# Delta-rule attention with a gated MLP on one core: triangular inverses in 16x16 blocks for the first three groups, weight decoding at a lower rank, more split buffers and held-back output products at the end

## The chip, the cores and the metric

The kernel runs on one core of a Trainium2 chip. A core has a matrix engine (TensorE, PE in the profile; its weight loads are PEld), a vector engine (VectorE, DVE), a scalar engine (ScalarE, ACT), GpSimd (POOL) and a queue processor that here issues all the transfers (SyncE, SP). The metric is the device time of one execution in microseconds. Shown are the median of three runs and, apart from it, one execution with a profile. Each engine works through its own list of instructions in order; an instruction that has to wait holds up all that stand behind it on its engine.

## The reference

```python
k_n = k / (np.linalg.norm(k, axis=-1, keepdims=True) + 1e-06)
for t in range(S):                       # S = 768; B, H, D = 4, 8, 48
    y[:, :, t] = q[:, :, t] @ state      # per head, state is 48 x 48
    v_old = state.T @ k_n[:, :, t]
    state = state + beta[t] * outer(k_n[:, :, t], v[:, :, t] - v_old)
x = y.transpose(0, 2, 1, 3).reshape(B, S, H * D)         # 4 x 768 x 384
h = np.maximum(x @ w_in, 0.0)                            # 384 -> 1024
u, v = h[..., :512], h[..., 512:]
v_n = (v - mean(v)) / np.sqrt(var(v) + 1e-06)
v_s = np.einsum('ts,bsd->btd', w_spatial, v_n) + b_spatial[None, :, None]
return (u * v_s) @ w_out                                 # 512 -> 384
```

(The inner products are written here as matrix products; in the reference they are `einsum`s over all heads.)

## The kernel before

**Recurrence.** The 768 positions are cut into 12 chunks of 64. Two batches with their 16 heads run at a time, so there are 24 steps: 0 to 11 for batches 0 and 1, 12 to 23 for batches 2 and 3. Inside a chunk, the recurrence is the inverse of a 64x64 unit triangular matrix per head, built from K K^T, the key norms and beta. Four steps form a group, and `prep(g)` prepares a group's inverses: matmuls `kk` (tile `ke`, or `bn` at the start), a copy into the tile `xt`, half copies (L402), a 32x32 block transpose on DVE into `la` (L407), small operations on 128x32 tiles for the norm (L413 to L422: `gd`, `sq`, `t0`, `nl`, `dv`), a scaling of `la` (L423), then the *lanes*. The lanes invert all the 32x32 triangular blocks of the group at once: one block a partition row, one column j after the other, each a product (L439) and a sum (L444) over all rows that are known so far. Rows 0 to 15 are DVE's (`ps`, in PSUM), rows 16 to 31 GpSimd's (`wl`). A copy (L450) and a transpose (L451) put the result back into `xt`. `widen(s)` then makes a 64x64 inverse of two 32x32 inverses and the block between them: a transpose `tn` (L470), 16 matmuls, a scaling `pi` (L487), 16 matmuls, two copies (L491). A matmul in f32 shows as two records in the trace, one in fp32r as one.

`step(s)` is the recurrence itself: the old value from the state (`s,bn`), a subtraction (L542), the product with the inverse (`bn,xt`), the copy `w` (L571), the product into the state (`w,bn`), its sum (L584) and the outputs (`bn,s` and `pt,w`). `kqt` makes the masked Q K^T (`pt`, L516), `scale_v` the scaled v (L502), and `load(s)` brings `bn` (k, q, v, k of a step, 896 KB) for one of two buffers.

**MLP.** Every second step finishes 128 rows of x for two batches. `convert` splits them into high and low parts; `mlp_v`, `norm_v`, `split_v` and `mlp_u` make v, its norm, its split into tiles `vf`, and u. `gate(b)` starts once a batch's 768 rows are there: for three column ranges `mlp_g` multiplies with w_spatial, adds the bias `bbc` (L735), multiplies with u (L738) and splits the result (L740, L741); `mlp_o` multiplies with w_out, and the result is copied (L756) and stored. Products of weights and data are three matmuls (high x high, high x low, low x high).

**Weights** arrive as 64-bit floats. `load_f64` decodes w_in in six blocks on DVE (L288, L294, L296), ACT (L290 to L293, L297) and GpSimd (L298, L299), and `split_w` splits them (L278, L279).

**The order** is written by a planner. `P.add(engine, duration, function, reads, writes, pr=...)` registers each operation; `run` takes operations one by one with planned durations: of the engine that can start earliest it takes the ready operation with the lowest rank `pr`. The emitted order is then each engine's list. Ranks: the recurrence has the step number (0 to 23), the widening 250 + s, kqt 300 + s, the MLP from 5000 on, prep of group 0 has -925 to -922, that of the later groups 1,000 + 100 g and more. Decoding on DVE has `pre(pr)`, -930, while the weights' rank is under 1000. Pools hand out buffers: `full` (six `vf` tiles), `raw` (seven), `g` (the gated tiles, `g0` and from step 23 on `xt0`, `xt1`), `pm` (PSUM banks).

Of the kernel before, what the change touches and what calls it, by code (L numbers as in the profile page):

```python
# [27 lines left out]
EPS = 1e-6  # L28
NRAW = 7
# [4 lines left out]
class Op:  # L34
    __slots__ = ("i", "eng", "dur", "fn", "pr", "deps", "out", "n", "acq", "rel", "give", "start", "end", "lag", "port")
# [15 lines left out]
class Plan:  # L51
# [35 lines left out]

    def run(self):
# [3 lines left out]
        est = {}  # L92
# [12 lines left out]
        while left:  # L105
# [36 lines left out]
            o.end = t + o.dur + o.lag  # L142
            for p, h in o.rel:
# [28 lines left out]
def delta_rule_gated_mlp(  # L172
# [21 lines left out]
    bbc = new("bbc", SEQ)  # L194
# [4 lines left out]
    ptm = [new(f"pt{i}", NS * 64) for i in range(2)]  # L199
    bnd = [new(f"bn{i}", 1792) for i in range(2)]  # L200
# [9 lines left out]
    la, wl, ke2 = (tagged(t, 1024) for t in ("la", "wl", "ke"))  # L210
# [3 lines left out]
    raw_ = lambda h: h.get(lambda u: tagged(f"vr{u}", DH))  # L214
    full_ = lambda h: h.get(lambda u: tagged(f"vf{u}", 2 * DH, F32R))
# [22 lines left out]
    P.pool("raw", range(NRAW))  # L238
    P.pool("full", range(NFULL))
# [17 lines left out]
    P.add("POOL", 1.0, lambda: nc.gpsimd.memset(wl, 0.0), wr=["wlo", "whi"], pr=-10)  # L257
# [43 lines left out]
    def pre(pr):  # L301
        return -930 if pr < 1000 else pr

    def weights():
        for idx in range(2 * NK):
# [3 lines left out]
            t1 = lambda h1=h1: h1.get(lambda u: tagged(f"vf{u}", 1024))  # L309
# [9 lines left out]
        ld(bbc, b_sp.unsqueeze(0).broadcast_to([128, SEQ]), wr=["bbc"], pr=950)  # L319
        for idx in range(NT // 2):  # L320
# [3 lines left out]
            ld(lambda t=t: v3(t()[:, 0:1536], SEQ), w_sp[idx * 256 : idx * 256 + 256].rearrange("(a p) n -> p a n", p=128), wr=[key], pr=900 + idx, acq=[("st", h)], lag=4.0)  # L324
# [32 lines left out]
    def prep(g):  # L357
        base = 1925 + g * 100 if g else 0
        for s4 in range(GP):
# [10 lines left out]
            ld(ke, k_t[s], wr=[kk_], pr=30 + s if g else -20 + s4)  # L370
# [7 lines left out]
            P.add("PE", 0.55, kk, rd=[kk_], wr=bk + [("kk", s)] + [("x", k % (2 * GP), q) for k in (range(s, s + GP) if s4 == 0 else (s,)) for q in ("d0", "o0", "z1", "d1")], pr=400 + s, acq=acq)  # L378
# [13 lines left out]
        ld(bl_[g % 2], b_l[g], wr=[("bl", g % 2)], pr=40 + g if g else -5)  # L392
# [11 lines left out]
        for a in range(2):  # L404
# [3 lines left out]
            out=v3(la, 32), in_=xg()[:, :, 0:32].rearrange("p b c -> p c b")), rd=xp("d0") + [("za", 0), ("za", 1)], wr=["la"] + xp("z1"), pr=base - 930)  # L408
        la3 = v3(la, 32)
# [3 lines left out]
        P.add("DVE", 0.1, lambda: nc.vector.tensor_copy(out=gd, in_=dg), rd=["la"], wr=["gd"], pr=p0, port=True)  # L413
# [13 lines left out]
        P.add("ACT", 0.2, lambda: nc.scalar.copy(out=pr_[:, 0 : 15 * 33 + 1 : 33], in_=dv[:, 0:16]), rd=["dv"], wr=["wp"], pr=p0)  # L427
        P.add("POOL", 0.15, lambda: nc.gpsimd.tensor_copy(out=wl[:, 16 * 33 : 31 * 33 + 1 : 33], in_=dv[:, 16:32]), rd=["dv"], wr=["whi"], pr=p0)
        P.add("DVE", 0.1, lambda: nc.vector.transpose(out=nn[g % 2], in_=n_l), rd=["nl"], wr=[("nn", g % 2)], pr=p0 + 1)
        w3, wp = v3(wl, 32), v3(pr_, 32)  # L430

        def lanes(eng, key, w, t_, i0, j):
# [5 lines left out]
            cost = dve_t(n * m) if eng == "DVE" else 0.1 + 1.85e-3 * n * m  # L438
# [349 lines left out]
    for s in range(NP):  # L788
# [9 lines left out]
        if s % GP == GP - 1 and g + 2 < NG:  # L798
            prep(g + 2)
# [69 lines left out]
```

## Time and profile before

| | us |
|---|---|
| median of 3 runs (555.1 to 558.07) | 557.56 |
| profiled execution, its own time | 559.17 |
| its span, first to last instruction | 557.5 |
| PE busy | 447.9 |
| DVE busy | 276.3 |
| ACT busy | 237.5 |
| POOL busy | 267.4 |

The span was at a mean granted TensorE clock of 0.916. Busy times of different engines overlap. A busy TensorE can still be slow: the clock that it was granted is a column of its own in the views by stage. In rows that list an instruction, the bracket at the end is the idle time of its engine just before it, and what ended that. In rows of groups, the busy total and the mean in ns come first, then the idle time before, and who ended it.

### The profile page before, as it was taken

The page shows a single profiled execution, that of the slowest core. Times are in us where ns is not written, and L with a number is a line of the kernel's source. Part 1 is how long each engine was busy: PE and PEld are TensorE (multiplying, and loading weights), DVE is VectorE, ACT ScalarE, POOL GpSimd, SP SyncE. Part 2 cuts the span into 40 slices and gives each one's busy share as a digit, 9 for nine tenths or more (in the row PEclk, how much of TensorE's full clock was granted, in tenths as well). Part 3 has the DMA queues.
Part 4 walks back from the last instruction along what each step waited for, and adds up shares of the span by engine and source line. Part 5 has one row for each costly group of instructions (what it writes and reads, how often), then busy time and mean ns, then how long its engine had stood idle before and what let it go on. Part 6 is the DMA issues. An engine that isn't in the chain of part 4 may idle for free.

```text
span 557.5 us, 19319 instructions
## 1 busy us (share of the span) xinstructions
PE 447.9 (80%) x8520; PEld 402.9 (72%) x8520; DVE 276.3 (50%) x690; ACT 237.5 (43%) x505; POOL 267.4 (48%) x372
## 2 busy tenths in 40 slices
PE   3000497959688998887979789898999997999996
PEld 3000496748677876777778679787999996998996
DVE  3599447688866489756887584213320021100100
ACT  3762642275428548664524213343323576014111
POOL 2189565758324466537456334344245141448442
PEclk9999999988869699885598798978999999899999
DMA  8601233321432363025302240210000000001001
GB/s 279 243 1 57 63 101 127 112 96 46 134 136 82 101 204 87 29 70 171 112 2 96 77 141 32 88 58 29 9 29 28 29 2 1 1 29 52 6 29 56
DMA packets 16020, 42.49 MB, mean 76 GB/s; under 512 B 3393, under 2 KB 7617, under 8 KB 15937
## 3 DMA queue, kind: packets, MB, share of 16 engines
q1 hardware_dynamic: 15936, 41.27, 22.4%
q8 instruction: 66, 1.08, 0.8%
q14 instruction: 18, 0.14, 0.1%
HBM read 35.36 MB, written 4.72 MB: 72 GB/s over the span
## 4 chain that ended last, share of the span: by engine, by line
PE 63%; DVE 20%; ACT 5%; issue 5%; DMA 4%; POOL 1%; SPq 1%; POOLq 0%; ACTq 0%; DVEq 0%
PE ps L355 63%; DVE ps L444 4%; DVE prod L439 4%; DMA bn<-in_bun 2%; DMA vf<-in_w_in 2%; DVE xt L451 2%; DVE pt L516 1%; DVE vf L296 1%; DVE la L407 1%; DVE ut L294 1%; ACT gt L653 1%; ACT vr L668 1%; ACT w L571 1%; SPq L250 1%; DVE la L423 1%
## 5 line engine op out<-in xcount | busy, mean ns | idle before, releaser
L355 PE MATMUL ps<-wsp_h,vf 128*128 128x256 f32 x576 | 122.4, 295 | 5.1 <-ACT vf L676 2.5
L355 PEld LDWEIGHTS ps<-wsp_h,vf 128*128 128x128 f32 x576 | 97.2, 196 | 7.7 <-ACT vf L676 2.7
L355 PE MATMUL ps<-wsp_l,vf 128*128 128x256 f32 x288 | 83.3, 289 | 0.0
L735 DVE TENSOR_TENSOR gt<-ps,bbc 128x512 f32<-128x512 f32 x24 | 16.6, 691 | 104.7 <-PE ps L355 104.7
L738 POOL TENSOR_TENSOR gt<-gt,ut 128x512 f32<-128x512 f32 x24 | 30.8, 1284 | 71.4 <-DVE gt L735 70.0
L444 DVE TENSOR_TENSOR ps<-ps,prod 128x192 f32<-128x192 f32 (+8 forms) x180 | 59.3, 329 | 5.4
L439 DVE TENSOR_TENSOR prod<-ps,la 128x192 f32<-128x192 f32 (+8 forms) x180 | 57.8, 321 | 5.4
L355 PEld LDWEIGHTS ps<-wsp_l,vf 128*128 128x128 f32 x288 | 56.7, 197 | 0.0
L677 POOL TENSOR_TENSOR vf<-vr,vf 128x512 fp32r<-128x512 f32 x24 | 30.6, 1288 | 51.0 <-ACT vf L676 51.0
L355 PE MATMUL ps<-ke 48*64 48x64 f32 x704 | 18.9, 262 | 41.2 <-DVE pt L516 38.4
L355 PEld LDWEIGHTS ps<-ke 48*64 48x64 f32 x704 | 15.7, 168 | 46.7 <-DVE pt L516 38.9
L355 PE MATMUL ps<-bn 48*64 48x64 f32 x832 | 23.7, 271 | 22.0 <-DVE pt L516 12.4
L502 POOL TENSOR_TENSOR bn<-bn,nn 128x384 f32<-128x384 f32 x24 | 20.9, 873 | 37.2 <-DMA bn<-in_bun 21.9
L355 PEld LDWEIGHTS ps<-bn 48*64 48x64 f32 x832 | 20.3, 179 | 24.4 <-DVE pt L516 12.7
L402 POOL COPY xt<-xt 32x1024 f32<-32x1024 f32 x17 | 17.6, 1035 | 40.4 <-DVE xt L451 20.8
L355 PE MATMUL ps<-wout_h,g 128*128 128x384 f32 x96 | 27.4, 348 | 3.0 <-ACT g L740 2.2
L584 DVE TENSOR_TENSOR s<-s,ps 112x384 f32<-112x384 f32 x20 | 11.0, 552 | 36.2 <-PE ps L355 32.9
L571 ACT COPY w<-ps 128x384 f32<-128x384 f32 x24 | 11.4, 477 | 41.1 <-PE ps L355 37.4
L756 ACT COPY ob<-ps 128x384 f32<-128x384 f32 x24 | 11.5, 478 | 41.0 <-PE ps L355 29.6
L355 PE MATMUL ps<-wout_h,xt 128*128 128x384 f32 x96 | 26.6, 343 | 2.1 <-POOL xt L741 1.5
L444 POOL TENSOR_TENSOR wl<-wl,prod 128x28 f32<-128x28 f32 (+3 forms) x84 | 23.8, 283 | 6.3
L439 POOL TENSOR_TENSOR prod<-wl,la 128x28 f32<-128x28 f32 (+3 forms) x84 | 23.1, 275 | 6.3
(142 smaller groups left out, 1099.4 us busy)
## 6 DMA issues: line engine op xcount, KB each, us to landing
bn<-in_bun SPq DMA_DIRECT2D x22, 896.0 KB, 4.7
ke<-in_k_t SPq DMA_DIRECT2D x22, 256.0 KB, 2.9
out<-ob SPq DMA_DIRECT2D x24, 192.0 KB, 1.9
vf<-in_w_in SPq DMA_DIRECT2D x6, 512.0 KB, 9.0
g<-in_w_sp SPq DMA_DIRECT2D x3, 768.0 KB, 4.4
g<-in_w_out SPq DMA_DIRECT2D x4, 384.0 KB, 3.2
bn<-in_bun SPq DMA_DIRECT2D x2, 640.0 KB, 6.3
xs<-xs SPq DMA_DIRECT2D x66, 16.0 KB, 3.1
```

What stands on the lines that cost most here:

```text
L355: nc.tensor.matmul(o, l, r, start=start, stop=stop)
L402: (nc.gpsimd.tensor_copy if eng == "POOL" else nc.scalar.copy)(out=xg()[r, :, o : o + 32], in_=xg()[r, :, i : i + 32])
L439: P.add(eng, cost, lambda: e.tensor_tensor(out=dst if j == i0 else pt, in0=w[:, :n, j : j + 1].broadcast_to([128, n, m]), in1=la3[:, j, j ...
L444: P.add(eng, cost, lambda: e.tensor_tensor(out=dst, in0=dst, in1=pt, op=ALU.add), rd=[pk], wr=[key], pr=p0 + 2)
L451: P.add("DVE", 2.2, lambda: nc.vector.transpose(out=xg()[:, :, 0:32].rearrange("p b c -> p c b"), in_=w3.rearrange("p i t -> p t i")), rd= ...
L502: P.add("POOL", 0.84, lambda: nc.gpsimd.tensor_tensor(out=v, in0=v, in1=n.unsqueeze(2).broadcast_to([128, NS, HD]), op=ALU.mult), rd=[("nn ...
L571: P.add("ACT", 0.48, lambda: nc.scalar.copy(out=v3(w, 192), in_=v3(pc, 512)[:, :, 0:192]), rd=["pc"], wr=[("w", s % 2)], pr=pr)
L584: P.add("DVE", 0.55, lambda: nc.vector.tensor_tensor(out=sv, in0=sv, in1=pv, op=ALU.add), rd=["pc"], wr=["S"], pr=pr)
L677: P.add("POOL", pool_t(512), lambda: nc.gpsimd.tensor_sub(out=full_(f)[:, DH : 2 * DH], in0=raw_(r), in1=full_(f)[:, 0:DH]), rd=[kk, ("vh" ...
L735: P.add("DVE", 0.69, lambda: nc.vector.tensor_tensor(out=gt(), in0=v3(bank(h.unit), 256), in1=bbc[:, th * 256 : th * 256 + 256].unsqueeze( ...
L738: P.add("POOL", pool_t(512), lambda: nc.gpsimd.tensor_mul(out=gt_[t.unit], in0=gt_[t.unit], in1=u_(uh)[:, half * 512 : half * 512 + 512]), ...
L756: P.add("ACT", 0.48, lambda: nc.scalar.copy(out=ob_[t.unit], in_=bank(h.unit)[:, :DM]), rd=[("po", b, th, o)], wr=[("ob", b, th, o)], pr=4 ...
```

## The change

- **16x16 lanes.** For the first three groups (`G16 = 3`) the lanes invert two 16x16 blocks of each row instead of one 32x32 block, all on DVE, with 15 columns instead of 31; GpSimd has no lanes there. The new `widen16(s)` makes the 32x32 inverses of them, per step, ahead of the old `widen(s)`. The group's half copies and memsets behind the lanes go; `widen16` does them per step. ACT copies the block that it needs into `kd` before it is overwritten. `kd` and `tn6` lie in the tile that later holds the bias, whose load moves behind step 11.
- **Decoding later.** `pre` gives -800 instead of -930.
- **The end.** When the last step is done, the two `bn` buffers join the pool `full` and the two `pt` buffers the pool `raw`. Batch 1's split waits for batch 0's gates as before; batch 3's split waits for batch 2's splits instead of batch 2's gates. Output products have a later rank: +135 for batch 1, +8 for batches 2 and 3, +2.5 before.
- **Replanned.** Planned durations are changed all over, transfers share a line of 330 KB a us, and the planner has a model of a TensorE that slows when it is little used. `prep(g + 1)` is registered at the start of group g, behind that group's `widen16`. Every engine's order can change.

```diff
     def pre(pr):
-        return -930 if pr < 1000 else pr
+        return -800 if pr < 1000 else pr
...
+        if g < G16:
+            P.add("ACT", 0.6, lambda: nc.scalar.copy(out=v3(kd, 16), in_=xg()[:, :, 0:16]), rd=xp("d0") + [("za", 0), ("za", 1)], wr=["kd"], pr=410 + g)
...
-        P.add("DVE", 0.1, lambda: nc.vector.tensor_copy(out=gd, in_=dg), rd=["la"], wr=["gd"], pr=p0, port=True)
+        P.add("DVE", 0.24, lambda: nc.vector.tensor_copy(out=gd, in_=dg), rd=["la"], wr=["gd"], pr=p0, port=True)
...
+        def lanes16(j):
+            n, m = j + 1, 15 - j
+            w4 = pr_.rearrange("p (h i t) -> p h i t", h=2, t=16)
+            pt = prod[:, : 2 * n * m].rearrange("p (h a b) -> p h a b", h=2, b=m)
+            dst = w4[:, :, :n, j + 1 : 16]
+            cost = 0.19 + 1.05e-3 * 2 * n * m
+            P.add("DVE", cost, lambda: nc.vector.tensor_tensor(
+                out=dst if j == 0 else pt, in0=w4[:, :, :n, j : j + 1].broadcast_to([128, 2, n, m]),
+                in1=v3(la_, 528)[:, :, 33 * j + 1 : 32 * j + 16].unsqueeze(2).broadcast_to([128, 2, n, m]), op=ALU.mult),
+                rd=["la", "wp"], wr=["wp"] if j == 0 else [("prod", "DVE")], pr=p0 + 2)
+            if j:
+                P.add("DVE", cost, lambda: nc.vector.tensor_tensor(out=dst, in0=dst, in1=pt, op=ALU.add), rd=[("prod", "DVE")], wr=["wp"], pr=p0 + 2)
...
+    def widen16(s):
...
+        P.add("DVE", 0.46, lambda: nc.vector.transpose(out=v3(tn6, 32), in_=x8_()[:, :, 0:32]), rd=zd, wr=["tn6"], pr=pr)
+
+        def e():
+            x8 = x8_()
+            for q in range(NS):
+                for k in range(4):
+                    r = slice(32 * k, 32 * k + 32)
+                    mm(pe[32 * k : 32 * k + 16, q * 16 : q * 16 + 16], kd[r, (b0 + q) * 16 : (b0 + q) * 16 + 16], x8[r, q, 16:32])
+
+        def f():
+            for q in range(NS):
+                for k in range(4):
+                    h = slice(32 * k, 32 * k + 16)
+                    mm(pe[32 * k : 32 * k + 32, 256 + q * 16 : 256 + q * 16 + 16], tn6[h, q * 32 : q * 32 + 32], gi[h, q * 16 : q * 16 + 16])
+
+        P.add("PE", 1.0, e, rd=["kd"] + zd, wr=["pe0"], pr=pr)
+        P.add("ACT", 0.26, lambda: nc.scalar.mul(out=gi, in_=pe[:, 0:128], mul=-1.0), rd=["pe0"], wr=["gi"], pr=pr)
+        P.add("PE", 1.0, f, rd=["gi", "tn6"], wr=["pe0"], pr=pr)
+        P.add("DVE", 0.29, lambda: nc.vector.tensor_tensor(
+            out=x8_()[:, :, 16:32], in0=x8_()[:, :, 16:32], in1=v3(pe[:, 256:384], 16), op=ALU.add), rd=["pe0"], wr=zd, pr=pr)
+        for a in range(2):
+            r = slice(a * 64 + 32, a * 64 + 64)
+            P.add("ACT", 0.37, lambda r=r: nc.scalar.copy(out=x8_()[r, :, 32:64], in_=x8_()[r, :, 0:32]), rd=[("x", sl, "z1")], wr=[("zb", s, a)], pr=pr)
+            P.add("POOL", 0.4, lambda r=r: nc.gpsimd.memset(x8_()[r, :, 0:32], 0.0), rd=[("zb", s, a)], wr=[("zc", s, a)], pr=pr)
...
         if s == NP - 1:
             P.add("X", 0.0, None, rd=[("xs", s // 2)], wr=["pc"], give=[("pm", k) for k in (0, 1, 2, 3, 4)] + [("g", "xt0"), ("g", "xt1")])
+            P.add("X", 0.0, None, wr=[("bn", i, q) for i in range(2) for q in "kqvn"], give=[("full", "bn0"), ("full", "bn1")])
+            P.add("X", 0.0, None, wr=[("pt", 0), ("pt", 1)], give=[("raw", "pt0"), ("raw", "pt1")])
...
-rd=[kk, ("gdone", i // NT - 1)], wr=[("vh", i)]
+rd=[kk] + ([("gdone", 0)] if i // NT == 1 else [("vh", 2 * NT + k) for k in range(NT)] if i // NT == 3 else []), wr=[("vh", i)]
...
-                mlp_o(b, th, o, pr + th * 2 + 2.5 + o * 0.2)
+                mlp_o(b, th, o, pr + th * 2 + (2.5, 135, 8, 8)[b] + o * 0.2)
...
-    prep(1)
     P.add("X", 0.0, None, wr=["pm67"])
     for s in range(NP):
         g = s // GP
+        if s % GP == 0:
+            for k in range(GP if g < G16 else 0):
+                widen16(s + k)
+            if g + 1 < NG:
+                prep(g + 1)
         widen(s)
...
-        if s % GP == GP - 1 and g + 2 < NG:
-            prep(g + 2)
+        if s == GP * G16 - 1:
+            load_bias()
```

More of the change, by code (lines that the diff above doesn't have):

```diff
@@ L34 @@
 class Op:
-    __slots__ = ("i", "eng", "dur", "fn", "pr", "deps", "out", "n", "acq", "rel", "give", "start", "end", "lag", "port")
+    __slots__ = ("i", "eng", "dur", "fn", "pr", "deps", "out", "n", "acq", "rel", "give", "start", "end", "lag", "port", "kb", "took")
 class Hold:
@@ L86, in add, with gate @@
         return o
+    def gate(self, o, t):
+        left, z = o.dur, t
+        while left > 1e-9:
+            k = int(z // GATE)
+            if k not in self.busy:
+                self.busy[k] = 0.0
+                u = self.busy.get(k - 1, 0.0)
+                if z > 100.0 and (u < 0.47 * GATE if k - 1 not in self.slow else u < 0.68 * GATE):
+                    self.slow.add(k)
+            f = 2.0 if k in self.slow else 1.0
+            d = min(left * f, (k + 1) * GATE - z)
+            d = max(d, 1e-6)
+            self.busy[k] += d
+            left -= d / f
+            z += d
+        o.took = z - t
     def run(self):
@@ L91, in run @@
         port = {"DVE": 0.0, "POOL": 0.0}
-        est = {}
+        est, line, self.busy, self.slow = {}, 0.0, {}, set()
         def arm(o):
@@ L142, in run @@
             o.end = t + o.dur + o.lag
+            if o.kb:
+                line = max(line, t) + o.kb / 330.0
+                o.end = max(line + o.lag, o.end)
+            if e == "PE":
+                self.gate(o, t)
+                free[e] = t + o.took
+                o.end = t + o.took
             for p, h in o.rel:
@@ L198, in delta_rule_gated_mlp @@
     tn, pi = new("tn", NS * 32), new("pi", NS * 32)
-    ptm = [new(f"pt{i}", NS * 64) for i in range(2)]
-    bnd = [new(f"bn{i}", 1792) for i in range(2)]
+    ptm = [sb.tile([128, NS * 64], F32, name=f"pt{i}", tag=f"pt{i}") for i in range(2)]
+    bnd = [sb.tile([128, 1792], F32, name=f"bn{i}", tag=f"bn{i}") for i in range(2)]
     wt = [new(f"w{i}", NS * HD) for i in range(2)]
@@ L237, in delta_rule_gated_mlp @@
     P.pool("x", [("xh", "xl")])
-    P.pool("raw", range(NRAW))
-    P.pool("full", range(NFULL))
+    P.pool("raw", [f"vr{i}" for i in range(NRAW)])
+    P.pool("full", [f"vf{i}" for i in range(NFULL)])
     P.pool("u", range(NU))
@@ L437, in lanes @@
             dst = w[:, :n, j + 1 : 32]
-            cost = dve_t(n * m) if eng == "DVE" else 0.1 + 1.85e-3 * n * m
+            cost = 0.19 + 1.05e-3 * n * m if eng == "DVE" else 0.27 + 1.75e-3 * n * m
             P.add(eng, cost, lambda: e.tensor_tensor(
@@ L453, in prep @@
             rd=["wlo", "whi"], wr=xp("d0") + xp("z1"), pr=p0 + 3)
+        if g < G16:
+            if g == G16 - 1:
+                P.add("POOL", 0.6, lambda: nc.gpsimd.memset(wl[:, 512:1024], 0.0), wr=["whi"], pr=p0 + 4)
+            return
         P.add("POOL", 0.6, lambda: nc.gpsimd.memset(wl[:, 512:1024], 0.0), wr=["whi"], pr=p0 + 4)
@@ L642, in mlp_v @@
         st = stt[:, J * 16 : J * 16 + 16]
-        P.add("ACT", 0.75, lambda: nc.scalar.activation(out=raw_(r), in_=bank(h.unit), func=AF.Relu, accum_out=st[:, j : j + 1]),
+        P.add("ACT", 0.82, lambda: nc.scalar.activation(out=raw_(r), in_=bank(h.unit), func=AF.Relu, accum_out=st[:, j : j + 1]),
               rd=[("pv", i)], wr=[("st", i), ("vr", i)], pr=400 + J, rel=[("pm", h)])
@@ L675, in split_v @@
         kk, q = ("vr", i), 440 + i
-        P.add("ACT", 0.6, lambda: nc.scalar.copy(out=full_(f)[:, 0:DH], in_=raw_(r)), rd=[kk, ("gdone", i // NT - 1)], wr=[("vh", i)], pr=q, acq=[("full", f)])
+        P.add("ACT", 0.6, lambda: nc.scalar.copy(out=full_(f)[:, 0:DH], in_=raw_(r)), rd=[kk] + ([("gdone", 0)] if i // NT == 1 else [("vh", 2 * NT + k) for k in range(NT)] if i // NT == 3 else []), wr=[("vh", i)], pr=q, acq=[("full", f)])
         P.add("POOL", pool_t(512), lambda: nc.gpsimd.tensor_sub(out=full_(f)[:, DH : 2 * DH], in0=raw_(r), in1=full_(f)[:, 0:DH]), rd=[kk, ("vh", i)], wr=[("vl", i)], pr=q, rel=[("raw", r)])
```

121 lines of the change are left out of this document (73 added, 48 removed).

## The prediction

> **What bounds the kernel now.** I read the slices of the span first, then the busy time by stage, then the two engines at the start in order of time, then the waits at the end. The slices (tenths busy, 13.9 us each) and the clock:
>
> ```profile
> span 557.5 us, 19319 instructions
> ...
> PE   3000497959688998887979789898999997999996
> ...
> PEclk9999999988869699885598798978999999899999
> ```
>
> TensorE is nearly idle for five slices, 80 to 90% busy at a varying clock up to slice 28, and full after that. The stages are cut at the gaps between groups of four steps; columns are length, then busy time (and instructions) of PE, weight loads, DVE, ACT, POOL, then the granted clock:
>
> ```profile
> 0.00:71.00 71.00, 13.89 (x420) 12.18 (x424) 45.44 (x100) 36.13 (x56) 38.22 (x65) 1.00 0.38 129
> 71.00:98.00 27.00, 23.39 (x800) 21.53 (x800) 17.27 (x43) 9.05 (x21) 14.93 (x20) 1.00 0.34 110
> 98.00:135.00 37.00, 31.12 (x435) 25.01 (x433) 29.37 (x79) 17.80 (x42) 26.04 (x45) 0.91 0.29 90
> 135.00:160.00 25.00, 18.74 (x778) 16.61 (x773) 19.71 (x54) 11.26 (x25) 11.37 (x26) 0.80 0.36 119
> 160.00:181.00 21.00, 19.75 (x532) 16.04 (x530) 12.51 (x34) 13.17 (x30) 6.28 (x7) 0.91 0.35 102
> 181.00:206.00 25.00, 23.36 (x710) 19.32 (x711) 15.33 (x39) 11.35 (x28) 13.36 (x28) 0.80 0.41 134
> 206.00:240.00 34.00, 28.60 (x474) 23.97 (x472) 26.27 (x72) 25.81 (x58) 19.08 (x26) 0.95 0.25 74
> 240.00:395.00 155.00, 135.54 (x3285) 120.48 (x3285) 87.06 (x214) 57.01 (x124) 71.14 (x108) 0.82 0.24 79
> 395.00:466.00 71.00, 71.00 (x519) 67.38 (x519) 13.75 (x38) 34.92 (x83) 27.34 (x20) 1.00 0.06 19
> 466.00:474.00 8.00, 4.71 (x38) 4.29 (x37) 1.32 (x8) 4.95 (x12) 1.27 (x1) 1.00 0.00 0
> 474.00:546.00 72.00, 70.68 (x523) 69.97 (x523) 7.61 (x11) 14.06 (x26) 35.81 (x28) 0.98 0.07 25
> 546.00:557.50 11.50, 7.11 (x38) 6.14 (x37) 0.69 (x1) 1.95 (x4) 2.55 (x2) 0.94 0.14 51
> ```
>
> After the recurrence (395 us) 160 us of MLP work are still queued on PE. So the recurrence doesn't set the end; the sum of PE's work does, plus what PE loses by waiting or by a low clock. I count as lost the stage's length less busy time times clock. The rows at the start show that the clock column misses something there:
>
> ```profile
> 63.11 1.06 PE L355 MATMUL ps<-tn,xt 32*32 32x32 f32 x32 [0.40 <-DVE tn L470]
> ...
> 70.91 1.10 PE L355 MATMUL ps<-bn,xt 64*64 64x48 f32 x32
> ...
> 125.18 0.69 PE L355 MATMUL ps<-tn,xt 32*32 32x32 f32 x32 [1.88 <-DVE tn L470]
> ...
> 240.05 0.69 PE L355 MATMUL ps<-xt,pi 32*32 32x32 f32 x32
> 240.67 0.57 PE L355 MATMUL ps<-w,bn 64*48 64x48 f32 x32
> 241.06 0.63 PE L355 MATMUL ps<-pt,w 64*48 64x64 f32 x32
> ```
>
> The same 32 records take 1.06 us at 63 and 0.69 us at 125: until about 105 us PE runs at 0.65 of its later pace although the column says 1.00. With 0.65 for 71 to 98, the losses are 27 - 23.4 x 0.65 = 12 us, then about 11 (98 to 135, partly slow), 10, 3, 6 and 7 up to 240 (49 in all), 44 from 240 to 395, and 3.3 + 2.7 + 4.8 = 11 behind that. Work from 71 us on is thus 486.5 - 104 = 383 us at full pace.
>
> **The change part by part.** *The start.* DVE, in order of time:
>
> ```profile
> 10.49 1.90 DVE L407 STREAM_TRANSPOSE la<-xt 128x1024 f32<-128x1024 f32 x1 [1.45 <-ACT xt L402]
> ...
> 21.08 0.43 DVE L288 TENSOR_SCALAR ut<-vf 128x512 uint32<-128x512 uint32 x1 [0.85 <-DMA vf<-in_w_in]
> 21.43 0.18 DVE L413 COPY gd<-la 128x32 f32<-128x32 f32 x1
> ...
> 27.55 0.20 DVE L439 TENSOR_TENSOR ps<-ps,la 128x31 f32<-128x31 f32 x1
> ...
> 46.07 0.28 DVE L444 TENSOR_TENSOR ps<-ps,prod 128x112 f32<-128x112 f32 x1
> 46.39 0.26 DVE L439 TENSOR_TENSOR prod<-ps,la 128x96 f32<-128x96 f32 x1
> ...
> 48.31 0.22 DVE L444 TENSOR_TENSOR ps<-ps,prod 128x48 f32<-128x48 f32 x1
> 48.43 0.72 DVE L294 SCALAR_TENSOR_TENSOR ut<-vf,ut 128x512 uint32<-128x512 uint32 x1
> ...
> 58.92 0.18 DVE L444 TENSOR_TENSOR ps<-ps,prod 128x16 f32<-128x16 f32 x1
> 60.35 2.23 DVE L451 STREAM_TRANSPOSE xt<-wl 128x1024 f32<-128x1024 f32 x1 [0.65 <-ACT wl L450]
> ```
>
> The transpose that feeds group 0 ends at 12.39, but its next reader runs at 21.43: the six first decode operations (L288) stand in front of it and wait for the w_in transfers. A second batch of decoding sits inside the lanes from 48.43 to about 58.3. The lower rank of the decoding (-800, behind -925) takes both out: 9.0 and 9.8 us. The lanes themselves take 27.55 to 48.5 and 0.8 more, 21.8 us. The 16x16 lanes are 15 products and 14 sums of 2(j+1)(15-j) elements, 1,360 for all products. From start to start 112 elements take 0.32 us (46.07 to 46.39), which is 0.04 over the duration; 48 elements then take 0.26, so the fit is 0.215 + 0.00094 n: 29 x 0.215 + 0.00094 x 2,690 (all products and sums) = 8.8 us, 13 less.
>
> So for group 0: 12.4; about 5 for the small operations (27.55 - 21.43 = 6.1 now, with pieces of decoding between), 17.5; lanes to 26.2; copy and transpose 3.5 as now (59.1 to 62.6), 29.7. Then the new widening to 32x32: two matmul blocks at the slow pace, 1.6 us each, and 2.1 us for the scaling, sum, copies and memset, 35; then the old widening, 4.5 without group 1's matmuls in between, 39.5. I take **40** for the matmul that is at 70.91 now: **-31** (bounds 36 and 46, since ACT and POOL have decode operations of 0.7 and 1.3 us that can stand ahead of each hop). The price of decoding later:
>
> ```profile
> 39.31 1.28 POOL L298 TENSOR_TENSOR ut<-ut,vf 128x512 f32<-128x512 f32 x1
> ...
> 98.03 1.22 PE L355 MATMUL ps<-win_h,xh 128*128 128x512 f32 x2
> ```
>
> POOL's part (18 operations of 1.3 us) starts at 39 now, behind the POOL lanes that group 0 loses; it can start near 18 and needs 23 us. Its results are read at 98 now, and not before two steps and the conversion of x then, near 62. So it is hidden; if it ends later than that, only MLP work that has no deadline waits. The bias load, moved behind step 11, is read only by the gates of the second half; on SP its wait stands before the next steps' loads, and I cost it at nothing.
>
> *Added matmuls.* widen16 has two blocks of 32 matmuls for each of 12 steps; two records each, so 64 records a block, 24 blocks. No row has this shape. From start to start, 32 records of the old widening take 0.62 us (240.05 to 240.67), and 32 of the four-tile block behind take 0.39. A block then costs 2 x 0.62 = 1.24 (at most 1.32 by the isolated 0.66), 0.78 by the four-tile pace, or 0.62 if half the columns halve the price. The new blocks use four tiles, but of 32 rows as the old widening: I take 1.0, **+24** (15 to 32). The Trainium skill ("TensorEngine Tiling (Array Packing)", Instruction Overhead) says that a matmul pays some 60 cycles whatever its free size and that no tiling should be taken from a size already small; it speaks against this change, and by it the block costs the 1.24, +30 in place of +24. The trace agrees in part: blocks of 32 and of 64 columns both come near 0.62, but the 48-column one goes at 0.39.
>
> *Added on the other engines.* Per step:
>
> ```profile
> L470 DVE STREAM_TRANSPOSE tn<-xt 128x256 f32<-128x256 f32 x24 | 10.6, 440 | 17.9 <-PE ps L355 17.6
> L487 ACT ACTIVATE pi<-ps 128x256 f32<-128x256 f32 x24 | 9.2, 382 | 13.5 <-PE ps L355 13.2
> L491 ACT COPY xt<-ps 32x256 f32<-32x256 f32 x48 | 17.3, 361 | 20.5 <-PE ps L355 20.0
> L458 POOL MEMSET xt<- 32x1024 f32 x12 | 11.5, 954 | 6.6 <-DVE tn L470 2.5 <-DVE gd L413 1.7 <-DVE st L650 1.4
> ```
>
> One more DVE transpose (0.44) and sum (about 0.3), one ACT scaling (under 0.38) and two copies of 0.36, two POOL memsets (at most 0.95 each). They replace the group's two half copies and two memsets. DVE is relieved all the same: 13 us less lanes a group against 3 more. These sit beside PE's work of a group, 33 to 46 us at full pace by the stages above (71 to 135, 135 to 181, 181 to 240); without that cover the chain costs as in the rival below. Behind each new wait stand, on PE, the step's own matmuls; on DVE, the next group's lanes; on POOL, the v scaling.
>
> *Groups 1 and 2.* From 98 to 135 the recurrence stands while DVE finishes group 1's lanes (109 to 120.6) and its transpose; 135 to 160 has the opposite fault, all recurrence and no filler, with the clock at 0.80. Lanes that are 13 us shorter let steps and MLP blocks mix. Of the 49 us lost I take **-10**: nothing at worst, 25 at best.
>
> *Waits for instructions, and the end.*
>
> ```profile
> PE ps L355 <- issue: 12.2, 10, 2.6
> ```
>
> ```profile
> 472.38 0.39 PE L355 MATMUL ps<-wsp_h,vf 128*128 128x256 f32 x1 [2.45 <-ACT vf L676]
> ...
> 550.82 0.62 PE L355 MATMUL ps<-wout_h,xt 128*128 128x384 f32 x2 [0.73 <-POOL xt L741]
> ```
>
> PE waited 12.2 us for nothing that the profile shows, and its longest such waits lie among small matmuls. 24 x 64 = 1,536 more records on 8,520 give 12.2 x 0.18 = 2.2; they fall into the same stretches, so **+3** (0 to 8). At the end, PE waits at 472 for batch 3's split v and at 550 for the last gated tile. With two more split buffers, two more raw ones and output products kept for those places, each batch has six products of 12 matmuls to stand in. Of the 11 us lost I take **-7** (-3 to -9, since the last product, its copy and its store stay). The held products of batch 1 become filler between 240 and 395; that, and planned durations nearer to the trace (small DVE operations 0.24 where 0.1 stood), works on the 44 us lost there. **-4** (-20 to +10): a plan made anew moves every wait, and nothing in the profile says which way.
>
> *The sum.* -31 + 24 - 10 + 3 - 7 - 4 = -25. From the profiled span of 557.5: 532.5. The profiled execution took 559.17, 1.67 more than its span, and the median of the runs shown is 557.56, so a span and a median have the same number here. Forecast **532.5**, with its own range from 518 to 546 (the bounds of start, matmuls and second half, not all at their ends together).
>
> **The rivals.**
>
> *The narrow matmuls cost as much as the wide ones, half of them at low pace.* For it: 32 and 64 columns cost the same above, and 71 to 98 runs at 0.65 with PE 23.4 of 27 us busy. A block is then 1.24 us at full pace and 2.1 at the other, 1.66 on average, 24 of them +40: the sum becomes -9, 548.5. Against it: the block at 0.39. The Trainium skill's rule ("TensorEngine Tiling (Array Packing)", Instruction Overhead), told above, would lead here.
>
> *DVE stays behind the transfers.* If the plan again puts a decode operation ahead of group 0's small ones, they start near 21 as now; 9 us of the 31 are lost: 541. The place is the first reader of the transposed tile. Against it stands the rank.
>
> *The plan frees the second half.* If the fillers close half of the 44 us lost, -22 in place of -4: 514.5. For it: the 395 to 466 stage shows PE full when only MLP work is left.
>
> *Slower: the widening comes into the chain of steps.* Its links (matmul, scaling, matmul, sum, copy, memset) share one tile each for kd, gi, tn6 and one PSUM bank, so one step's must end before the next's starts. By the rows: 1.0 + 0.4 + 1.0 + 0.3 + 0.7 + 0.95 = 4.4 us, 12 times, 52 us, if each starts only when its step needs it. Then the recurrence's first half takes 52 more, PE has no filler since the gates need all twelve steps, and in place of +24 and -10 stands +52: -31 + 52 + 3 - 7 = +17, 574.5. It decides where less than 4.4 us of other PE work lies between two steps. Against it: 33 to 46 us of PE work a group stand there against 4 x 4.4, and the links need nothing from the step before.
>
> *Nothing comes of the early start* would need the recurrence not to feed PE earlier. Since 383 us of work wait from 71 on, and lost time there is 104, I see no room for it.
>
> **How the numbers follow.** Forecast 0.60; equal price 0.15; DVE behind the transfers 0.07; second half freed 0.11; slower 0.07. The range reaches from the freed half to the equal price and a little past both: **511 to 552**; it leaves out the slower rival and the tails, some 0.15. A measurement of this kernel tells about 0.5% from no change, 554.8 to 560.3. Faster 0.60 + 0.07 + 0.11 and 0.11 of the equal price: 0.89. The same: 0.03 of the equal price and 0.01 of the slower rival: 0.04. Slower: 0.07.
>
> **What would show it.** The first reader of the transposed tile before 14 us and the first `bn,xt` matmul near 40: the start. 64-record blocks of 1.0 us at full pace: the added matmuls; 1.24 and 2.1 are the first rival. Gaps between groups (98 to 135 now) of under 15 us: the lanes. Less than 5 us lost behind the recurrence, with output products where the waits were: the end. PE under 80% in the first half, waiting for ACT, DVE or POOL operations of the widening, would be the slower case. The forecast fails if steps begin at 40 but the first half still ends near 206, the early start given back.

## The result, and the profile after

| | before | after |
|---|---|---|
| median, us (4 runs each) | 556.75 | 533.66 |
| range, us | 555.1 to 558.07 | 531.87 to 536.48 |
| profiled execution, us | 559.17 | 533.54 |
| its span, us | 557.5 | 531.7 |
| ratio after/before, 95% interval | | 0.959 (0.954 to 0.964) |

The kernel is 4.1% faster. The forecast was 532.5, the measured median 533.66. The number was right. Of the terms behind it, the added matmuls came near, the start did so only when it is counted as idle time, the end came as forecast, and two others came far from where they were put and cancelled each other. The medians of e7, e9 and e12 further down are over four runs of which one was slow (999.63, 684.53 and 555.47 us); their other runs alone have medians of 544.02, 538.98 and 546.6, and the ratios leave the slow ones out.

The first view is the page of the kernel after: its span, its engines and its slices.

```profile
span 531.7 us, 22308 instructions
...
PE 461.5 (87%) x10056; PEld 413.4 (78%) x10056; DVE 240.3 (45%) x618; ACT 247.0 (46%) x541; POOL 237.4 (45%) x295
...
PE   4336978989799898888598899999999999999997
...
PEclk9999999995955969989699799989999999999999
```

PE starts earlier and is 90% busy or more from slice 24 to the last but one, with no hole at slice 34 as before. It is 13.6 us longer busy (447.9 before). The clock column is lowest (5) at slices 10, 12 and 13, in the first half. The second view is the kernel after, by stage, cut at its own gaps between groups. Columns are those of the stage view of before.

```profile
49.00:74.00 25.00, 22.32 (x766) 20.57 (x764) 18.25 (x45) 13.74 (x28) 14.87 (x12) 1.00 0.36 119
74.00:108.00 34.00, 29.88 (x962) 24.60 (x955) 13.76 (x36) 16.90 (x40) 17.07 (x19) 1.00 0.32 99
108.00:139.00 31.00, 27.61 (x804) 21.98 (x797) 19.48 (x51) 14.18 (x32) 6.10 (x6) 0.78 0.30 96
139.00:172.00 33.00, 28.40 (x951) 23.48 (x953) 11.76 (x25) 18.50 (x42) 13.47 (x18) 0.59 0.29 90
172.00:206.00 34.00, 29.01 (x812) 23.87 (x805) 21.64 (x63) 17.19 (x42) 12.27 (x21) 0.85 0.33 110
206.00:243.00 37.00, 32.94 (x498) 27.69 (x499) 28.02 (x86) 24.56 (x59) 23.47 (x41) 0.95 0.20 58
243.00:373.00 130.00, 115.52 (x3272) 102.29 (x3268) 72.63 (x182) 52.11 (x113) 61.95 (x95) 0.92 0.28 91
373.00:531.70 158.70, 155.12 (x1140) 150.72 (x1137) 21.57 (x58) 55.46 (x126) 66.80 (x51) 1.00 0.07 24
```

The stage from step 12 to step 23 is the row of 130 us; it was 155 us long before, at a clock of 0.82. The last row has lost only 3.6 us.

To place the gain I took each step's copy `w` as a mark (its start in the timelines of ACT) and split PE's time between marks in windows of 3.4 us: idle; busy time times (1 - granted clock), called low clock; and the rest, called work. Each cell is length = idle + low clock + work, in us; other cuts of the windows move a term by up to 0.3.

| stage | before | after | difference |
|---|---|---|---|
| to step 0's copy | 72.1 = 57.1 + 0 + 15.0 | 50.4 = 28.3 + 0 + 22.1 | -21.7 |
| step 0 to step 12 | 167.3 = 24.1 + 15.4 + 127.8 | 192.3 = 23.8 + 24.8 + 143.7 | +25.0 |
| step 12 to step 23 | 155.0 = 19.4 + 23.7 + 111.9 | 129.1 = 14.5 + 7.5 + 107.0 | -25.9 |
| behind step 23 | 163.1 = 9.0 + 1.5 + 152.6 | 160.0 = 3.6 + 0 + 156.4 | -3.1 |
| the whole span | 557.5 = 109.6 + 40.6 + 407.3 | 531.7 = 70.2 + 32.3 + 429.2 | -25.8 |

The zeros of low clock in the first row are the column's, and the column misses something. These rows of the kernel after are the same 32 records at three times, in stretches granted 1.00, 1.00 and 0.50:

```profile
46.37 1.06 PE L385 MATMUL ps<-xt,pi 32*32 32x32 f32 x32 [0.48 <-ACT pi L553]
...
105.44 0.69 PE L385 MATMUL ps<-xt,pi 32*32 32x32 f32 x32
...
125.09 1.06 PE L385 MATMUL ps<-xt,pi 32*32 32x32 f32 x32
```

Until about 97 us (105.5 before) PE runs at the pace that it has at a granted 0.50. It is busy for 62 us up to there, 45 before, and by the table's own rule half of that, 31 and 22 us, is low clock that the table counts as work; this is an estimate.

Step 11's copy starts at 205.18 before and at 205.16 after. **The whole early start is gone by the middle of the kernel.** Up to step 12 PE idles 29.1 us less, but works 23.0 longer and has 9.4 more of low clock. With the estimate for the slow start, that is some 14 us of work, near the price of the new matmuls, and some 18 of low clock: a PE that starts earlier is busy for longer at the slow pace. In this plan the net gain stands in the 26 us of the second half, where the lanes weren't changed at all, and 3 at the end.

### The profile page after: what moved, and what is told of

It reads as the page before. It is cut to its first block, busy times and chain, and to the rows that moved or that the text cites. A ratio compares the mean times of both kernels' runs of the same rounds, so it can differ in the third digit from the quotient of the medians.

```text
span 531.7 us, 22308 instructions
## 1 busy us (share of the span) xinstructions
PE 461.5 (87%) x10056; PEld 413.4 (78%) x10056; DVE 240.3 (45%) x618; ACT 247.0 (46%) x541; POOL 237.4 (45%) x295
## 4 chain that ended last, share of the span: by engine, by line
PE 75%; DVE 8%; ACT 7%; issue 6%; DMA 1%; POOL 1%; SPq 1%; DVEq 0%; ACTq 0%; POOLq 0%
PE ps L385 75%; DMA vf<-in_w_in 1%; DVE ps L479 1%; DVE xt L506 1%; DVE prod L474 1%; ACT gt L752 1%; DVE ps L492 1%; DVE prod L487 1%; ACT vr L767 1%; SPq L281 1%; ACT ut L321 1%; ACT ut L323 0%; ACT xt L557 0%; ACT w L668 0%; DVE pt L613 0%
## 5 line engine op out<-in xcount | busy, mean ns | idle before, releaser
L385 PE MATMUL ps<-wsp_h,vf 128*128 128x256 f32 x480 | 97.1, 287 | 0.0
L385 PEld LDWEIGHTS ps<-wsp_h,vf 128*128 128x128 f32 x480 | 78.0, 190 | 1.4
L385 PE MATMUL ps<-wsp_l,vf 128*128 128x256 f32 x240 | 68.0, 284 | 0.0
L385 PEld LDWEIGHTS ps<-wsp_l,vf 128*128 128x128 f32 x240 | 45.5, 190 | 0.1
L776 POOL TENSOR_TENSOR vf<-vr,vf 128x512 fp32r<-128x512 f32 x19 | 24.4, 1298 | 24.1 <-ACT vf L775 23.9
L479 DVE TENSOR_TENSOR ps<-ps,prod 128x192 f32<-128x192 f32 (+13 forms) x90 | 29.6, 329 | 2.7
L557 ACT COPY xt<-ps 32x256 f32<-32x256 f32 x48 | 17.4, 362 | 29.0 <-PE ps L385 28.3
L474 DVE TENSOR_TENSOR prod<-ps,la 128x192 f32<-128x192 f32 (+13 forms) x90 | 28.9, 321 | 2.6
L719 POOL TENSOR_TENSOR xl<-xs,xh 128x768 fp32r<-128x768 f32 x9 | 16.5, 1832 | 29.5 <-ACT xh L718 27.9
L432 POOL COPY xt<-xt 32x1024 f32<-32x1024 f32 x14 | 14.5, 1034 | 28.9 <-ACT xt L412 12.1
L385 PE MATMUL ps<-xt,pi 32*32 32x32 f32 x768 | 20.5, 209 | 7.6 <-issue 7.1
L385 PEld LDWEIGHTS ps<-xt,pi 32*32 32x32 f32 x768 | 17.2, 123 | 12.0 <-issue 8.8
L385 PEld LDWEIGHTS ps<-bn 48*64 48x64 f32 x832 | 19.4, 174 | 8.6 <-issue 4.2
```

The costliest lines, as they stand in the source:

```text
L385: nc.tensor.matmul(o, l, r, start=start, stop=stop)
L432: (nc.gpsimd.tensor_copy if eng == "POOL" else nc.scalar.copy)(out=xg()[r, :, o : o + 32], in_=xg()[r, :, i : i + 32])
L474: P.add(eng, cost, lambda: e.tensor_tensor(out=dst if j == i0 else pt, in0=w[:, :n, j : j + 1].broadcast_to([128, n, m]), in1=la3[:, j, j ...
L479: P.add(eng, cost, lambda: e.tensor_tensor(out=dst, in0=dst, in1=pt, op=ALU.add), rd=[pk], wr=[key], pr=p0 + 2)
L557: P.add("ACT", 0.37, lambda r=r: nc.scalar.copy(out=x8_()[r, :, 32:64], in_=v3(pe[r, 256:512], 32)), rd=["pe0"], wr=[("fo", s, a)], pr=pr)
L719: P.add("POOL", pool_t(768), lambda: nc.gpsimd.tensor_sub(out=xA(x)[1], in0=xs_(xo)[:, 0:768], in1=xA(x)[0]), rd=ks_ + [("xs", J), ("xh", ...
```

## The experiments

The theory after the result (A in the expectations): the early start is paid back by the new matmul blocks on a PE that is already full, and what is gained comes from the end and from a second half that happens to be ordered better. The rivals: the short lanes and the early start are worth their time (B); the new planned durations made the second half; the held products made it. Every experiment is timed against the kernel before on its own chip.

| run | median, us | ratio to before (95%) | first `w` | steps 12 to 23 |
|---|---|---|---|---|
| the change | 533.66 | 0.959 (0.954 to 0.964) | 50.4 | 129.1 |
| e1, 16x16 in group 0 only | 542.62 | 0.973 (0.966 to 0.980) | 52.1 | 138.5 |
| e2, no 16x16 | 536.38 | 0.961 (0.954 to 0.968) | 53.9 | 141.4 |
| e3, replanned alone | 555.22 | 1.000 (0.996 to 1.004) | 61.1 | 138.9 |
| e4, products not held | 539.81 | 0.966 (0.960 to 0.973) | 51.1 | 131.3 |
| e5, widen16 step by step | 559.46 | 1.011 (1.004 to 1.019) | 43.0 | 161.9 |
| e6, blocks planned as measured | 543.70 | 0.983 (0.973 to 0.994) | 50.2 | 147.2 |
| e7, replanned with the end | 545.66 | 0.986 (0.972 to 1.000) | 63.4 | 136.6 |
| e8, no 16x16, old rank | 544.05 | 0.983 (0.977 to 0.990) | 61.1 | 139.8 |
| e9, the change, nudge 1 | 539.73 | 0.969 (0.961 to 0.976) | 52.3 | 145.1 |
| e10, the change, nudge 2 | 529.07 | 0.952 (0.944 to 0.961) | 50.4 | 141.7 |
| e11, no 16x16, nudge 1 | 537.42 | 0.968 (0.962 to 0.974) | 53.7 | 139.8 |
| e12, no 16x16, nudge 2 | 548.16 | 0.985 (0.977 to 0.992) | 53.5 | 147.5 |

### e1 and e2: less or nothing of the 16x16 lanes

```diff
-G16 = 3
+G16 = 1
```

> The changed kernel with 16x16 lanes for group 0 alone: 8 of the 24 new matmul blocks stay, groups 1 and 2 have 32x32 lanes again. Theory A (the early start was paid back by the new matmul blocks, their instruction waits and the low clock around them): steps still begin near 49 us, step 11 ends 5 to 15 us before 205, and the time is 520 to 530 us. Theory B (the short lanes are what keeps groups 1 and 2 on time, and the blocks are cheap): steps begin near 49, the gaps ahead of steps 4 and 8 grow by about 10 us each, and the time is 537 to 550 us.

```diff
-G16 = 3
+G16 = 0
...
-        if s == GP * G16 - 1:
+        if s == 0:
             load_bias()
```

> The changed kernel without any 16x16 lanes (the bias is loaded behind step 0). Theory A: the first step comes 8 to 10 us later than 49, since the lanes of group 0 take 13 us more and four per-step widenings go, the first half ends at or before 205 all the same, and the time is 523 to 534 us. Theory B: the start is later and the gaps are longer, 540 to 555 us.

Neither theory as it stood. e1's time lies in B's range, but its steps do what A said, and more: with the lanes in group 0 only, step 11 comes at 187.9, 17 us earlier than after. Then group 3 isn't ready: step 12 is at 257.0. The rows are of e1, the waits of PE between 187 and 258 us (total, times, longest):

```profile
PE ps L385 <- DVE tn L536: 17.1, 1, 17.1
PE ps L385 <- ACT vr L742: 4.8, 1, 4.8
PE ps L385 <- ACT xh L718: 4.3, 1, 4.3
```

PE stands 17 us for a transpose that waits behind group 3's lanes. A lead of the recurrence is of no use when DVE's next group doesn't lead as well. e2, without any 16x16 lanes, is 3 us above the change, 2 us past A's range and below B's, and its first step is only 3.5 us later. One plan is compared with another here; e9 to e12 weigh that.

### e3, e7 and e4: the durations, and the end

e3 is the kernel after with these parts set back: no 16x16 lanes, rank -930, output products at +2.5, the old buffers, the old split rule and the old places of `prep` and of the bias load. What remains is the planner's durations and models. e7 adds the end again, with the new split rule, which this cut leaves out:

```diff
-                mlp_o(b, th, o, pr + th * 2 + 2.5 + o * 0.2)
+                mlp_o(b, th, o, pr + th * 2 + (2.5, 135, 8, 8)[b] + o * 0.2)
...
+            P.add("X", 0.0, None, wr=[("bn", i, q) for i in range(2) for q in "kqvn"], give=[("full", "bn0"), ("full", "bn1")])
+            P.add("X", 0.0, None, wr=[("pt", 0), ("pt", 1)], give=[("raw", "pt0"), ("raw", "pt1")])
```

> The kernel before with the new planned durations, the shared transfer line and the clock model alone: no 16x16 lanes, decoding at the old rank, old ranks of the output products, old buffers. If the plan made with the new durations is what shortened the second half, steps 12 to 23 take 130 to 138 us instead of 155 and the time is 535 to 545 us. If it was the held-back products and buffers, they take 150 to 160 us and the time is 550 to 560 us.

> The replanned kernel of e3 (no 16x16, old rank of decoding) with the held-back products, the extra buffers and the new split rule. If the end is what makes the second half and the tail shorter, 537 to 545 us against 555.2. If it is worth only the waits at the end, 549 to 553 us.

e4 is the change with the products at +2.5 again, all else kept:

> The changed kernel with all output products at the old rank (+2.5). If the held-back products of batch 1 are the filler that shortened the second half, steps 12 to 23 take over 145 us instead of 129, and the time is 545 to 555 us. If they only cover the waits at the end, the second half keeps within 5 us of 129 and the waits at the end come back, 3 to 7 us: 537 to 541 us.

Replanning alone, in this one plan, is worth nothing: ratio 1.000. Its first step is 11 us earlier and its steps 12 to 23 are 16 us shorter, close to what was expected of a good plan, but its steps 0 to 12 take 187.4 us against 167.3, and the time is the old one. An early start that is lost in a longer first half is there without the 16x16 lanes too.

Behind step 23, idle time and low clock are 10.8 + 2.5 us in e3 and 3.5 + 0 in e7, so the end is worth 9.8 us there. The medians differ by 9.6, the ratios by 1.4%, near 8 us; e7 is at the edge of its first case. Without the held products alone, e4 has 8.2 + 1.6 against 3.6 + 0 in the change, 6.2 us, and its time is 6.1 us longer: its second case. PE's waits behind step 23, first in e3, then in e4:

```profile
PE ps L386 <- ACT vf L774: 4.5, 1, 4.5
PE ps L386 <- POOL xt L839: 1.5, 2, 0.7
PE ps L386 <- ACT xt L838: 0.6, 1, 0.6
PE ps L386 <- POOL vf L775: 0.6, 1, 0.6
```

```profile
PE ps L385 <- ACT vf L775: 2.1, 1, 2.1
PE ps L385 <- POOL xt L840: 1.6, 2, 0.8
PE ps L385 <- POOL vf L776: 0.9, 1, 0.9
```

In e7 and in the kernel after, the same view lists no wait at all; the idle time that is left there is that of the last copy and store. This is the part of the change whose mechanism is shown: in all kernels that hold the products back the idle time there is 3.5 to 3.8 us. The held products aren't what shortens the second half: it is 131.3 us without them.

### e8: the rank of the decoding

From e2:

```diff
-        return -800 if pr < 1000 else pr
+        return -930 if pr < 1000 else pr
```

> The kernel of e2 (no 16x16 lanes, else changed) with the decoding back at -930. If the early start through the rank is worth its time, the first step's copy w comes near 61 us instead of 53.9 as in e3, and the time is 542 to 546 us against 536.4. If the start is given back in the first half, the first step is as late and the time stays within 3 us of 536.4.

The first step is 7.2 us later and the time is 7.7 us longer: the first case. But the three kernels without 16x16 lanes and with the new rank (e2, e11, e12) have 536.4, 537.4 and 548.2, so one plan with the old rank doesn't settle the size. That the rank brings the first step forward is clear: its copy is at 53.5 to 53.9 in those three.

### e5: the start alone, earlier still

```diff
-        if s % GP == 0:
-            for k in range(GP if g < G16 else 0):
-                widen16(s + k)
-            if g + 1 < NG:
-                prep(g + 1)
+        if g < G16:
+            widen16(s)
+        if s % GP == (GP - 1 if g < G16 else 0) and g + 1 < NG:
+            prep(g + 1)
         widen(s)
```

> The changed kernel with each widen16 registered directly ahead of its step's widen, instead of all four ahead of the group, so that step 0 needn't stand behind the three later ones (they share one PSUM bank, gi and tn6); the next group's prep is registered behind the fourth. If an earlier start is worth what it brings, the first step's copy w comes near 40 us instead of 50.4 and the time falls by 6 to 10 us: 523 to 528. If the first half is bound by PE work, waits and clock and not by its start, the first step is 8 to 11 us earlier, step 11 ends within 5 us of 205, and the time stays at 530 to 537.

PE's start in order of time, first after, then in e5:

```profile
29.71 0.73 PE L385 MATMUL ps<-xt,bbc 32*16 32x16 f32 x64 [3.49 <-DVE xt L506]
30.86 1.05 PE L385 MATMUL ps<-gi,bbc 16*32 16x16 f32 x64 [0.41 <-ACT gi L581]
32.95 0.73 PE L385 MATMUL ps<-xt,bbc 32*16 32x16 f32 x64 [1.04 <-DVE xt L583]
...
43.29 1.05 PE L385 MATMUL ps<-gi,bbc 16*32 16x16 f32 x64 [1.18 <-ACT gi L581]
44.82 1.06 PE L385 MATMUL ps<-tn,xt 32*32 32x32 f32 x32 [0.48 <-DVE xt L583]
...
49.26 1.10 PE L385 MATMUL ps<-bn,xt 64*64 64x48 f32 x32
```

```profile
31.53 0.73 PE L385 MATMUL ps<-xt,bbc 32*16 32x16 f32 x64 [3.46 <-DVE xt L506]
32.67 1.05 PE L385 MATMUL ps<-gi,bbc 16*32 16x16 f32 x64 [0.41 <-ACT gi L581]
34.67 1.06 PE L385 MATMUL ps<-tn,xt 32*32 32x32 f32 x32 [0.96 <-DVE tn L536]
...
40.29 1.10 PE L385 MATMUL ps<-bn,xt 64*64 64x48 f32 x32
```

After, four `widen16` (eight blocks) run before the first old widening; all use the same PSUM tile, so the order of registration fixes that. In e5 only one stands there, and the first `bn,xt` comes at 40.29 instead of 49.26. The time is 559.5 us, 26 longer. Step 11 comes at 215.1, ten us later than after. By the column, the low clock takes 68.6 us in e5 against 32.3 after, in the same split as above; that is more than the whole difference. Neither case fits: nine us of start didn't carry over, and the new order did worse than either theory had. `prep` is registered later here, so e5 doesn't say that an early start harms; it says that it isn't enough.

### e6, e9 to e12: the same work in another order

e6 changes two planned durations:

```diff
-        P.add("PE", 1.0, e, rd=["kd"] + zd, wr=["pe0"], pr=pr)
+        P.add("PE", 0.63, e, rd=["kd"] + zd, wr=["pe0"], pr=pr)
...
-        P.add("PE", 1.0, f, rd=["gi", "tn6"], wr=["pe0"], pr=pr)
+        P.add("PE", 0.67, f, rd=["gi", "tn6"], wr=["pe0"], pr=pr)
```

> The changed kernel with the new matmul blocks planned at 0.63 and 0.67 us, as they measure, instead of 1.0. The work is the same; only the order is planned anew. It shows how much a plan moves by chance: if the plan itself decides little, within 3 us of 533.7; if the gains hang on the accident of a plan, 5 us or more either way.

e9 (from the change) and e11 (from e2) change the planned issue of a transfer:

```diff
-    SPD = 0.55
+    SPD = 0.56
```

> The changed kernel with the planned time of a transfer's issue at 0.56 us instead of 0.55: nothing else, the same work in a slightly other order. With e6 and e10 it shows how far the time hangs on the plan. If 533.7 was a typical plan, 530 to 538 us; if it was a lucky one, 538 to 546, with the difference in the low clock and not in the work or the start.

> The kernel of e2 (no 16x16 lanes) with the nudge of e9. If the 16x16 lanes are worth something of their own, all plans without them lie above all plans with them: 540 us or more. If they only trade waits for work, 532 to 542 us, mixed with the plans of the changed kernel.

e10 (from the change) and e12 (from e2) change the planned hand-over from PE:

```diff
-    LAT = {"PE": 0.2, "DVE": 0.06, "ACT": 0.08, "POOL": 0.08, "SP": 0.0, "X": 0.0}
+    LAT = {"PE": 0.21, "DVE": 0.06, "ACT": 0.08, "POOL": 0.08, "SP": 0.0, "X": 0.0}
```

> The changed kernel with the planned hand-over from the matrix engine at 0.21 us instead of 0.20: the second nudge. Typical plan: 530 to 538 us. Lucky plan: 538 to 546.

> The kernel of e2 (no 16x16 lanes) with the nudge of e10; the same two cases: 540 us or more, or 532 to 542.

A hundredth of a microsecond in the planner moves the kernel by up to 6 us with the 16x16 lanes (529.1, 533.7, 539.7; with e6, 543.7) and by up to 12 without them (536.4, 537.4, 548.2). e9 falls into the range of a lucky plan, e10 below both of its ranges, e11 into the mixed case and e12 into the other. The instructions are the same; the order isn't. The second half, from step 12 to 23, in e6:

```profile
240.00:387.00 147.00, 134.63 (x3289) 120.31 (x3287) 77.59 (x187) 53.01 (x114) 65.72 (x94) 0.80 0.24 81
```

Beside the 130 us row of the kernel after: 17 us longer at a clock of 0.80 against 0.92. In the split, idle is 12.4 us against 14.5, and work 110.0 against 107.0; low clock is 24.8 against 7.5. So the change's short second half belongs to its plan and not to a part of the change: the three other plans of the same kernel have 141.7, 145.1 and 147.2. Nor is a short second half what makes a kernel fast: e10, the fastest, has 141.7 there and gains its time before step 12 (233.8 us against 242.7) and behind step 23 (151.5 against 160.0).

With the lanes the four ratios average 0.966, without them the three average 0.971. The difference of 0.5% is smaller than either spread: **whether the 16x16 lanes are worth anything in time stays open.** What they do to PE is clearer, since there the plans agree. The split up to step 12, in us:

| plans | idle | low clock | work |
|---|---|---|---|
| with the lanes (the change, e4, e6, e9, e10) | 52 to 58 | 16 to 28 | 160 to 167 |
| without them (e2, e11, e12) | 74 to 77 | 26 to 29 | 143 to 144 |

**The lanes take some 21 us of idle time off PE and put some 20 us of matmul time, part of it at the slow pace, in its place.** About 10 of the idle time go ahead of step 0 and the rest between steps 0 and 12.

e10 at 529.07 is the fastest kernel here, 5% under the one before; its interval overlaps the change's. With the parts added one after the other, the ratios are 1.000 (e3, replanned), 0.986 (e7, the end), 0.983 (e8, the places of `prep` and of the bias load), 0.961 (e2, the rank) and 0.959 (the lanes). Each comes from one plan, and of these steps only the end has its time found again in the trace.

## Why the prediction was right, and where it wasn't

The sum came out right (532.5 against 533.66; span 531.7), in part by luck: the -10 of the first half came as +9.1 in idle time and low clock, the -4 of the second as -21.1, and the two misses cancelled. The condition that the prediction gave for its failure, steps that begin at 40 and a first half that still ends near 206, was met in its second part, and the time fell all the same. Of the signs that it named, the first reader of the transposed tile runs at 12.62, so DVE doesn't stay behind the transfers, and less than 5 us are lost at the end; the gap ahead of step 4 isn't under 15 us.

- **The start: -31 predicted, -21.7 measured.** The working was right as far as it went: lanes expected from 17.5 to 26.2 run from 18.24 to 26.70, the transposed result expected at 29.7 is there at 29.69. The step that failed is "then the new widening", which counted one `widen16` ahead of the first old one where four stand. e5 has one there, and the first `bn,xt` comes at 40.29, where the prediction had 40. Ahead of step 0, idle time fell by 28.8 us and work rose by 7.1, which is those eight blocks (four of 0.73 us and four of 1.05). The sum has all blocks in its +24, so as idle time the term was nearly met.
- **That a microsecond of start is one of time.** This assumption under the sum held only in part. Step 11 has no lead left: what the start saved was spent by step 12 on the new matmuls, which the sum has, and on low clock, which it hasn't, 9.4 us by the column and some 18 with the slow start. e5's start nine us earlier doesn't test it, since that plan also loses 36 us more to low clock.
- **Added matmuls: +24 predicted; the two block rows of the kernel after sum to 21.4 us.**

```profile
L385 PE MATMUL ps<-gi,bbc 16*32 16x16 f32 x768 | 12.4, 204 | 8.1 <-ACT gi L581 5.5 <-issue 2.6
L385 PE MATMUL ps<-xt,bbc 32*16 32x16 f32 x768 | 9.0, 185 | 7.0 <-DVE xt L506 4.0 <-DVE xt L583 2.0 <-issue 1.0
```

```profile
99.69 0.69 PE L385 MATMUL ps<-xt,bbc 32*16 32x16 f32 x64
100.31 0.62 PE L385 MATMUL ps<-xh,win_l 128*128 128x256 f32 x3
...
101.56 0.73 PE L385 MATMUL ps<-gi,bbc 16*32 16x16 f32 x64
102.22 0.63 PE L385 MATMUL ps<-xh,win_l 128*128 128x256 f32 x3
```

  The second fence is PE's timeline after, at its full pace: 64 records take 0.62 us from start to start, half of the 1.24 that was the rival's price; a block of the other kind takes 0.66 (101.56 to 102.22). The rival of equal price is refuted for this shape: the records go at 9.7 ns each, where those of the old widening go at 19.4. The Trainium skill ("TensorEngine Tiling (Array Packing)", Instruction Overhead) says not to take a tiling from a size that is already small; the price that the prediction worked out from that isn't what these blocks cost. They have half the columns and twice as many row groups at once, and no run separates the two. Over the span a block takes 0.89 us (21.4 for 24), since part of them run at the slow pace.
- **Groups 1 and 2: -10 predicted; the first half got 25 us longer.** The reading that failed is that the gap of 98 to 135 is DVE's. It shrank from 39.8 to 35.5 us (step 3's copy to step 4's), with PE idle for 6.4 us of it before and 4.7 after. PE spends it on the MLP blocks of the steps ahead. A long distance between steps isn't a wait if the engine that sets the end is busy in it. From step 0 to 12, idle time stayed (24.1 to 23.8), work rose by 15.9 and low clock by 9.4. Most of that low clock lies between steps 4 and 8: 18.8 us, where it was 5.8. Against the plans without lanes the term has its sign right: they idle 36 to 38 us between steps 0 and 12.
- **Waits for instructions: +3 predicted, +9.2 measured.** The row of the kernel after, against 12.2 before:

```profile
PE ps L385 <- issue: 21.4, 20, 3.8
```

  The size failed, the cause fits: kernels with the lanes in three groups have 14.6 to 25.3 us of these waits, those without them 4.3 to 10.4.

- **The end: -7 predicted; 9.0 + 1.5 lost before, 3.6 + 0 after, -6.9.** Right, for the reason given, and shown by e3, e7 and e4.
- **The second half: -4 predicted (at best -20), -25.9 measured** between the marks, 21.1 of it in idle time and low clock. The rival "the plan frees the second half" is what happened, beside the others. The prediction said that nothing in the profile told which way a new plan would go. e6, e9 and e10 support that, and make the 25.9 a piece of luck, outside the prediction's own range for it.
- **The slower rival** (the widening comes into the chain of steps) is seen at the start only: PE waits 5.5 us for `gi`, all of it among the blocks before step 0.

What stays open: what in an order of PE's instructions makes the clock fall, and so why one plan loses 7.5 us to it in the second half and another 24.8.

## What to carry to other kernels

When one engine is full to the end, count a change in that engine's idle time, clock and work over the whole span; a stage that starts or ends earlier isn't yet a gain. When an order is planned anew, nudge the plan by something that means nothing and time it again before putting a gain down to a part of the change: here that alone moves the kernel by up to 12 us, and a part that is worth less can't be judged from one plan. Terms that the plans agree on can still be read: the idle time and the work up to step 12 kept the kernels with and without the lanes apart, where their times didn't. What did carry over is work kept back for the places where the full engine has nothing else to do.

## What the runs showed of the hardware that was not expected

The clock can stay low while PE is busy. Rows of the kernel after, PE busy of 10 us in the third column:

```profile
120.00:130.00 10.00, 10.00 (x207) 7.62 (x200) 5.48 (x19) 2.86 (x7) 0.83 (x1) 0.50 0.34 106
150.00:160.00 10.00, 8.96 (x352) 7.62 (x349) 3.03 (x6) 5.04 (x11) 2.86 (x6) 0.50 0.27 70
300.00:310.00 10.00, 10.00 (x344) 8.52 (x333) 8.67 (x24) 4.02 (x10) 6.58 (x19) 1.00 0.54 163
```

Ten busy microseconds at 0.50 in the first row and ten at 1.00 in the third. And the column can read 1.00 where the pace is that of 0.50: for the first 97 us of this kernel, as the rows behind the split show. The Trainium skill ("TensorE: Matmul & The Clock Gate", What's actually happening) has the full clock after one busy window of some 3.4 us; the first row disagrees, as far as the profile's busy time shows activity. By the column, low clock takes 32.3 us of the change's span, 40.2 of e6's and 68.6 of e5's, with the same matmuls in each. And the narrow matmuls of 16 columns on four row groups go at 9.7 ns a record; the next of the small ones, `w,bn` of 48 columns, go at 12.2 (32 records in 0.39 us, rows of the prediction).
